# Decayed keys and the diagonal of the first two chunks from the transposed r and k, by TensorE

## The chip, the cores and the metric

The program runs on one core of a Trainium2 chip. The metric is the device time of one execution in microseconds (us), median of several; lower is better. The core has TensorE (PE; its weight loads are PEld), VectorE (DVE), ScalarE (ACT), GpSimd (POOL), and SyncE (SP), which here only issues DMAs. Each engine works through its own instructions in the order in which the program writes them and waits on semaphores for the others.

## The reference

Three blocks in a row, all in float32:

```
# 1: attention with decay; batch 2, heads 8, seq 768, head_dim 48
for t in range(S):
    cur = einsum('bhd,bhe->bhde', u * k_t, v_t)
    y_t = einsum('bhd,bhde->bhe', r_t, state + cur)
    state = w * state + einsum('bhd,bhe->bhde', k_t, v_t)
# 2: mixture of experts on x = y as 1536 tokens x 384; 4 experts, 384 -> 1024 -> 384
p = domain_probs / (domain_probs.sum(-1) + 1e-9)
out = sum over e of p[:, e] * (relu(x @ w1[e]) @ w2[e])
# 3: one layer 384 -> 2048 -> 384 with ELU between
```

## The kernel before

The 1536 tokens are 12 chunks of 128, six for each batch. Of a chunk the kernel holds r and k transposed (`rkT`: 112 partitions, that is two heads of 48 at partitions 0 and 64, by 4 pairs of heads by 128 tokens), and r, k (`rk`) and v with the tokens on the partitions. Two tables of powers of the decay w, `T` and its reciprocal `Kd`, turn r and k into r·wᵗ and k·w⁻ᵗ (`s1h`, DVE, line 200). TensorE forms all products of k' and r' of a chunk (`s2`, line 252), DVE copies those under the mask into the tile `A` (`s2p`, line 259), and the diagonal of `A` is the sum over d of r·u·k for each token and head. In chunks 2 and later POOL writes that diagonal into `A` (`s1d`, line 235); for chunks 0 and 1 `A` holds zeros there, and v times the diagonal (`va`, line 230) is added by a product with the identity (line 362).

`s1u` (lines 217, 219) multiplies r, u and k of `rk` for the diagonal, `s1d` sums it (line 226). `s1k` (line 210) makes the decayed keys `kp` with the tokens on the partitions, from `rk` and `Kt`, the transposed `Kd` (`setup_kt`). `s3u` (line 273) multiplies `kp` with v for the state and `s3s` (lines 294, 296) brings the state forward on DVE. `s3` is the output of chunks 2 and later: a part from the state (line 308), `s3u`, and `A` times v (line 316). Chunks 0 and 1 go by `s3f` (line 359), which yields their outputs transposed, in PSUM, ready for the first layer; `put_x` splits them into a high part (ACT, line 477) and a low part (DVE, line 478).

Each float32 matrix of the layers is split so as well: `split` casts a slice of 128x768 weights on ACT (line 514) and subtracts on DVE (line 515), and then asks for the next load. `work(budget)` runs such pieces, `weights` runs them when one is missing. `layers` runs all experts; expert 0 goes over blocks of 256 tokens, and the attention of chunks 2 to 11 is laid between its steps: a list `steps`, of which `NS[f]` are taken behind step f of the first block. Each step f is: first layer (`st1`, line 664, nine products in 1.08 us), evacuation (`evac`, lines 676 and 677), steps of the list, second layer of the step two before (`st2`, line 702), one piece of `work`. Slice 2 is used first by step f = 2.

Ahead of `layers`, `fast` writes out by hand the order of zeros for TensorE (`warm`), loads, tables and the work on chunks 0 to 2. `probs` (POOL, lines 621 to 624), `probs2` (one reciprocal on DVE, line 629, and a product on POOL), `probs_out` (a transpose on TensorE, a copy, a store `pd`) and `load_pb` (a load of `pd` spread over 128 partitions, `pb`) bring the expert weights; `pb` is used first at line 720, where the results of a block leave PSUM. SP issues nearly all DMAs.

Of the kernel before, what the change touches and what calls it, by code (L numbers as in the profile page):

```python
# [34 lines left out]
WARM = 18  # L35
NS = (3, 1, 1, 1, 1, 1, 1, 2)
# [14 lines left out]
class Fast:  # L51
# [7 lines left out]
    def __init__(self, g, ctx):  # L59
        self.g, nc, tc = g, g.nc, g.tc  # L60
        self.c = ctx.enter_context(tc.tile_pool(name="at_c", bufs=1))
        self.p2 = ctx.enter_context(tc.tile_pool(name="at_2", bufs=2))
        self.p3 = ctx.enter_context(tc.tile_pool(name="at_3", bufs=3))
        self.p4 = ctx.enter_context(tc.tile_pool(name="at_4", bufs=4))
        self.ps = ctx.enter_context(tc.tile_pool(name="at_ps", bufs=1, space=PSUM))
        c = self.c
        self.A = [c.tile([P, 2, NP, P], F32, name=f"A{i}") for i in range(2)]
        self.kp = [c.tile([P, NP, 2, 64], F32, name=f"kp{i}") for i in range(2)]
        self.Sb = [c.tile([P, NP, 2, 64], F32, name=f"S{i}") for i in range(2)]
        self.wd = c.tile([P, NP], F32, name="wd")  # L70
# [3 lines left out]
        self.ub = c.tile([P, DM], F32, name="ub")  # L74
        self.vp = c.tile([P, 112 + 160 * H], F32, tag="xs", name="vp")
        self.Sp = c.tile([P, 96 + 192 * NP], F32, tag="yT", name="Sp")
        self.mask = c.tile([P, P], U8, name="mask")
        self.rkT, self.rk, self.v, self.va, self.pa, self.st = ({} for _ in range(6))
# [42 lines left out]
    def setup_loads(self):  # L121
        g, nc = self.g, self.g.nc
        nc.sync.dma_start(out=self.wd, in_=g.wd)
        for ci in range(2):
            self.load_T(ci)
            self.load_T2(ci, 0)
            self.load_T2(ci, 1)
        self.load_rk(0)
        nc.sync.dma_start(
            out=self.ub,  # L130
            in_=g.u.rearrange("h d -> (h d)").rearrange("(o n) -> o n", o=1).broadcast_to([P, DM]))
        self.load_v(0)
        self.load_rk(1)
        self.load_v(1)

    def setup_tables(self):
        g, nc = self.g, self.g.nc
        c = self.c
        zz = c.tile([P, 32], F32, name="zz")
        wf = c.tile([P, NP], F32, name="wf")  # L140
        nc.vector.memset(zz, 0.0)
        nc.vector.memset(self.T[:, :, 0:1], 1.0)
# [12 lines left out]
    def setup_tables2(self):  # L155
        nc, Kd = self.g.nc, self.Kd
        for n in (16, 32, 64):
            nc.gpsimd.tensor_tensor(
                out=Kd[:, :, n:2 * n], in0=Kd[:, :, 0:n],
                in1=Kd[:, :, n - 1:n].to_broadcast([P, NP, n]), op=ALU.mult)  # L160

    def setup_masks(self):
# [9 lines left out]
    def setup_zeros(self):  # L172
        nc = self.g.nc
        for t in self.A:
            for j in range(2):
                nc.scalar.copy(t[:, j].rearrange("s p t -> s (p t)"), self.zero)
        for i in range(0, self.vp.shape[1], 512):
            t = self.vp[:, i:min(i + 512, self.vp.shape[1])]
            nc.scalar.copy(t, self.zero[:, 0:t.shape[1]])

    def setup_rest(self):
        nc = self.g.nc
        for t in self.kp:
            nc.gpsimd.memset(t.rearrange("t p j d -> t (p j) d")[:, :, D:64], 0.0)
        nc.gpsimd.memset(self.Sp, 0.0)
        for t in self.Sb:
            nc.gpsimd.memset(t, 0.0)
# [35 lines left out]
    def s1d(self, ci):  # L223
        nc = self.g.nc
        a0 = self.p2.tile([P, H], F32, tag="a0", name="a0")
        nc.vector.tensor_reduce(out=a0, in_=self.st[ci]["uk"], axis=AX.X, op=ALU.add)  # L226
        if ci < 2:

# [4 lines left out]
            return  # L233
        for j in range(2):
            nc.gpsimd.tensor_tensor(  # L235
                out=self.A[ci % 2][:, j], in0=self.g.ident.rearrange("s (a t) -> s a t", a=1).to_broadcast([P, NP, P]),
                in1=a0.rearrange("s (p j o) -> s p j o", j=2, o=1)[:, :, j].to_broadcast([P, NP, P]), op=ALU.mult)

# [5 lines left out]
    def s2(self, ci):  # L244
# [4 lines left out]
        for p, j in ([(p, j) for j in range(2) for p in range(NP)] if ci < 2 else  # L249
                     [(p, j) for p in range(NP) for j in range(2)]):  # L250
# [48 lines left out]
    def s3(self, ci, more=False):  # L299
# [11 lines left out]
        pu = self.s3u(ci)  # L311
        for p in range(NP):
# [29 lines left out]
    def s3f(self, ci):  # L342
        g, nc = self.g, self.g.nc
        st = self.st.pop(ci)
        self.px = px = self.bank().rearrange("q (k t) -> q k t", k=4)
        for kk in range(KD):
# [9 lines left out]
            for n in range(max(map(len, ops))):  # L356
                for i, o in enumerate(ops):
                    if n < len(o):
                        nc.tensor.matmul(
                            px[64 * i:64 * (i + 1), kk, :], *o[n], start=not n and not kk, stop=False)  # L360
        for kk in range(KD):
            nc.tensor.matmul(
                px[:, kk, :], self.va[ci][:, kk * P:(kk + 1) * P], g.ident, start=False, stop=kk == KD - 1)

    def s3x(self, ci):
        self.g.put_x(0, ci * P, P, self.px[:, 0:KD, :], self.g.nc.vector)
# [93 lines left out]
class Gen:  # L460
# [11 lines left out]
    def put_x(self, j, o, n, src, eng):  # L472
# [4 lines left out]
        nc.scalar.copy(xh, src)  # L477
        eng.tensor_tensor(out=xl, in0=src, in1=xh.bitcast(F32), op=ALU.subtract)  # L478
# [28 lines left out]
    def split(self):  # L507
# [6 lines left out]
        nc.scalar.copy(hi, t)  # L514
        self.weng.tensor_tensor(out=lo, in0=t, in1=hi.bitcast(F32), op=ALU.subtract)  # L515
# [254 lines left out]
    def setup(self, ctx):  # L770
# [14 lines left out]
        self.later = []  # L785
# [49 lines left out]
    def fast(self):  # L835
        tc, nc = self.tc, self.nc
        with ExitStack() as ctx:
# [4 lines left out]
            at.warm(WARM)  # L842
            at.setup_zeros()
            at.setup_loads()
            dp = self.probs_in()
# [5 lines left out]
            at.setup_rest()  # L851
            at.setup_tables2()

# [6 lines left out]
            at.s1h(0, 0)  # L860
            at.s1h(0, 1)
            at.setup_kt()
            at.s2(0)
            at.s3v(0)
            at.s1h(1, 0)
            at.s1h(1, 1)
            at.s2p(0)
            at.s1u(0, nc.vector)
            at.s1k(0)
            self.probs(dp)  # L870
            at.s1u(1)
# [4 lines left out]
            load(3)  # L876
            at.s1d(0)
            self.probs2(dp)
            at.s2(1)
            pu = at.s3u(0)  # L880
            at.s3f(0)
            at.s2p(1)
            at.s3s(0, pu)
            at.s1k(1)
            at.s1u(2)
            at.load_rk(3)
            at.s1d(1)
            at.s3v(1)
            at.s3x(0)
            at.s1h(2, 0)  # L890
            at.s1h(2, 1)
            self.work(0.1)
            at.nbank = 0
            self.probs_out(at.bank)
            at.nbank = len(at.own)
            at.s3f(1)
            at.nbank = 2
            pu = at.s3u(1)
            at.s3x(1)
            at.s3s(1, pu)  # L900
            at.s1k(2)
            at.s1d(2)
            self.work(0.1)
            at.banks, at.nbank = at.own, 0
            load(4)
            at.load_rk(4)

# [157 lines left out]
```

## Time and profile before

| | |
|---|---|
| median of 3 runs | 658.91 us (658.71 to 659.19) |
| profiled execution | 658.46 us, of which the span from its first to its last instruction is 656.6 us |
| granted TensorE clock, mean | 0.994 of full |
| first product of the layers begins | 19.00 us |
| end of the last product | some 651 us, then evacuation and store |

Times in rows are us from the start of the span. A timeline row has the start, the time from the first start to the last end of the instructions merged in it, the engine, the line, what is written from what, shapes, the count, and in brackets how long the engine had been idle before, and on whom it waited. A busy share tells nothing of the order: the first 50 us, in which the attention, the loads and the splits start together, are read by themselves.

### The profile page before, as it was taken

The numbers are of one execution on the slowest core, as the hardware profiler recorded it, in microseconds if no ns is written. First come the engines' busy times: TensorE is split into PE (matmuls) and PEld (weight loads), VectorE is DVE, ScalarE is ACT, GpSimd is POOL, SyncE is SP. The second block draws the span as 40 slices with busy tenths as digits, with TensorE's granted clock in tenths as the row PEclk, the third lists the DMA queues.
The fourth block names the chain that finished last, engine by engine and source line by source line (L and its number), as shares of the span: only waits on it lengthen the run. The fifth ranks groups of instructions, "written<-read, shape, count | busy, mean of one in ns | idle before, by whom it ended". The sixth has DMA issues, their size and how long they took to land.

```text
span 656.6 us, 8916 instructions
## 1 busy us (share of the span) xinstructions
PE 646.6 (98%) x3563; PEld 545.5 (83%) x3563; DVE 342.1 (52%) x490; ACT 211.9 (32%) x351; POOL 213.1 (32%) x177
## 2 busy tenths in 40 slices
PE   8899999999999999999999999999999999999996
PEld 6799999988888888888888888888888888888885
DVE  7985677245454555554545455566666653112122
ACT  4331222233211123221122112123546464544441
POOL 6755575100012130312130314142764434333331
PEclk8899999999999999999999999999999999999999
DMA  8883661433320214322307132208540342001011
GB/s 251 252 251 138 177 177 50 145 118 99 121 67 29 96 60 158 107 111 96 97 0 265 68 125 97 96 25 311 193 145 26 119 144 97 0 1 48 1 49 53
DMA packets 27876, 73.26 MB, mean 112 GB/s; under 512 B 3170, under 2 KB 8723, under 8 KB 27827
## 3 DMA queue, kind: packets, MB, share of 16 engines
q1 hardware_dynamic: 23072, 60.00, 28.3%
q10 hardware_dynamic: 4754, 12.61, 5.0%
q8 instruction: 30, 0.49, 0.3%
q14 instruction: 20, 0.16, 0.1%
HBM read 55.67 MB, written 16.93 MB: 111 GB/s over the span
## 4 chain that ended last, share of the span: by engine, by line
PE 93%; DMA 2%; DVE 2%; POOL 1%; issue 1%; SPq 0%; ACT 0%; DVEq 0%
PE po L702 45%; PE ph L664 45%; PE pa L316 1%; DMA rk<-in_rkv_dram 1%; DMA ub<-in_u_dram 1%; PE pa L308 1%; PE po L252 1%; POOL A L235 1%; PE pa L252 0%; PE pa L273 0%; DVE acc L752 0%; DVE A L259 0%; POOL uk L217 0%; SPq L110 0%; DVE rkT L200 0%
## 5 line engine op out<-in xcount | busy, mean ns | idle before, releaser
L702 PE MATMUL po<-hh,wh 128*128 128x512 f32 (+1 forms) x480 | 177.4, 370 | 0.0
L702 PE MATMUL po<-hh,wl 128*128 128x512 f32 (+1 forms) x480 | 176.5, 368 | 0.0
L702 PE MATMUL po<-hl,wh 128*128 128x512 f32 (+1 forms) x480 | 176.5, 368 | 0.0
L664 PE MATMUL ph<-xh,wh 128*128 128x512 f32 (+1 forms) x480 | 175.0, 370 | 0.2
L664 PE MATMUL ph<-xh,wl 128*128 128x512 f32 (+1 forms) x480 | 174.4, 369 | 0.2 <-DVE wl L515 0.2
L676 ACT ACTIVATE hh<-ph 128x512 fp32r<-128x512 f32 (+1 forms) x112 | 60.1, 536 | 278.6 <-PE ph L664 275.1
L677 DVE SCALAR_TENSOR_TENSOR hl<-ph,hh 128x512 fp32r<-128x512 f32 (+1 forms) x112 | 68.5, 613 | 154.5 <-ACT hh L676 154.1
L664 PE MATMUL ph<-xl,wh 128*128 128x512 f32 (+1 forms) x480 | 125.0, 369 | 0.0
L664 PEld LDWEIGHTS ph<-xh,wh 128*128 128x128 f32 x480 | 90.8, 189 | 15.9 <-ACT xh L477 0.5
L702 PEld LDWEIGHTS po<-hh,wh 128*128 128x128 f32 x480 | 90.4, 188 | 16.2 <-issue 0.4
L664 PEld LDWEIGHTS ph<-xh,wl 128*128 128x128 f32 x480 | 90.9, 189 | 15.3 <-DVE wl L515 0.4
L702 PEld LDWEIGHTS po<-hl,wh 128*128 128x128 f32 x480 | 90.4, 188 | 15.1
L702 PEld LDWEIGHTS po<-hh,wl 128*128 128x128 f32 x480 | 90.4, 188 | 14.9
L689 POOL TENSOR_TENSOR hl<-g,hh 128x512 fp32r<-128x512 f32 x48 | 63.4, 1321 | 117.0 <-ACT hh L688 108.8
L664 PEld LDWEIGHTS ph<-xl,wh 128*128 128x128 f32 x480 | 86.2, 189 | 15.2 <-DVE xl L478 0.2
L686 DVE SCALAR_TENSOR_TENSOR g<-m,ph 128x512 f32<-128x512 f32 x48 | 33.0, 687 | 105.2 <-ACT m L684 101.0
L577 POOL TENSOR_TENSOR nl<-a,wide 128x768 fp32r<-128x768 f32 x16 | 30.1, 1883 | 173.5 <-DVE a L576 132.6
L724 POOL TENSOR_TENSOR acc<-acc,t 128x512 f32<-128x512 f32 x27 | 34.2, 1294 | 72.9 <-DVE t L723 72.9
L688 ACT CAST hh<-g 128x512 fp32r<-128x512 f32 x48 | 29.8, 622 | 42.9 <-DVE g L686 42.9
L683 ACT ACTIVATE m<-ph 128x512 f32<-128x512 f32 x48 | 28.7, 597 | 43.4 <-PE ph L664 35.9
L515 DVE TENSOR_TENSOR wl<-raw,wh 128x768 fp32r<-128x768 f32 x32 | 31.7, 1002 | 3.4 <-ACT wh L514 2.8
L235 POOL TENSOR_TENSOR A<-ident,a 128x512 f32<-128x512 f32 x20 | 23.1, 1177 | 27.2 <-DVE a L226 26.0
(105 smaller groups left out, 500.4 us busy)
## 6 DMA issues: line engine op xcount, KB each, us to landing
raw<-in_ws_dram SPq DMA_DIRECT2D x32, 384.0 KB, 4.4
wide<-in_ws_dram SPq DMA_DIRECT2D x16, 768.0 KB, 4.9
w<-nh ACTq DMA_DIRECT2D x16, 384.0 KB, 2.3
w<-nl ACTq DMA_DIRECT2D x16, 384.0 KB, 5.6
wh<-w SPq DMA_DIRECT2D x16, 384.0 KB, 5.5
wl<-w SPq DMA_DIRECT2D x16, 384.0 KB, 6.5
rk<-in_rkv_dram SPq DMA_DIRECT2D x12, 384.0 KB, 6.5
rkT<-in_rkT_dram SPq DMA_DIRECT2D x10, 448.0 KB, 6.1
```

Source lines behind the costliest of these rows:

```text
L235: nc.gpsimd.tensor_tensor(out=self.A[ci % 2][:, j], in0=self.g.ident.rearrange("s (a t) -> s a t", a=1).to_broadcast([P, NP, P]), in1=a0.r ...
L515: self.weng.tensor_tensor(out=lo, in0=t, in1=hi.bitcast(F32), op=ALU.subtract)
L577: nc.gpsimd.tensor_tensor(out=lo, in0=af, in1=cf, op=ALU.add)
L664: nc.tensor.matmul(ph[:, 0:n], a[:, kk, c0:c0 + P], b[:, kk], start=q == 0, stop=q == 3 * KD - 1)
L676: nc.scalar.activation(hh[:, 0:n], ph[:, 0:n], AF.Relu)
L677: nc.vector.scalar_tensor_tensor(out=hl[:, 0:n], in0=ph[:, 0:n], scalar=0.0, in1=hh[:, 0:n].bitcast(F32), op0=ALU.max, op1=ALU.subtract)
L683: nc.scalar.activation(m, ph, AF.Relu, scale=-1.0)
L686: nc.vector.scalar_tensor_tensor(out=gg, in0=m, scalar=-1.0, in1=ph, op0=ALU.add, op1=ALU.max)
L688: nc.scalar.copy(hh, gg)
L689: nc.gpsimd.tensor_tensor(out=hl, in0=gg, in1=hh.bitcast(F32), op=ALU.subtract)
L702: nc.tensor.matmul(po, a[:, ff, i * P:(i + 1) * P], b[:, 0:n], start=f == 0 and q == 0 and not i * n % TB, stop=f == NF - 1 and q == 2 and ...
L724: nc.gpsimd.tensor_tensor(out=a, in0=a, in1=t[:, 0:n], op=ALU.add)
```

## The change

- Chunks 0 and 1 no longer load `rk`. Their decayed keys are transposes of k' by TensorE, copied by ACT (`s2k`). Their diagonal: POOL multiplies r' and k' (`s1p`), TensorE multiplies that with u·w (`uw`) into a row for each head (`s2a`), ACT copies it, TensorE turns it back (`s2b`). `kp` of chunk 0 no longer needs `Kt`.
- u comes as one row, spread by a product with ones (`setup_ub`); one more small load, `uf`, stands before the loads of `rkT`.
- `T` is doubled by POOL and `Kd` by DVE, the other way round than before. `A[0]` is cleared by DVE, other clears go from POOL to ACT.
- The order ahead of `layers` is written anew. The loads of chunks 2 and 3 are asked for before the first product; `setup_kt`, `s1k(2)`, `probs` and `probs2` stand behind `s1d(2)`, at the end; `probs_out` moves among the steps, before `load_pb(0)`; the state of chunk 1 (`u1`) moves to the first step, so that `NS[0]` is 4 and not 3. The first slice of weights is split in two pieces and the second slice only in the steps: two slices before, one now.
- Zeros for TensorE: 10 and not 18 at the start, one and two between products of chunks 0 and 1, four and three in `s3` of chunks 2 and 3 (`WAIT`).

```diff
-WARM = 18
-NS = (3, 1, 1, 1, 1, 1, 1, 2)
+WARM = 10
+WAIT = {2: 4, 3: 3}
+NS = (4, 1, 1, 1, 1, 2, 1, 2)
...
         for n in (32, 64):
-            nc.vector.tensor_tensor(
+            nc.gpsimd.tensor_tensor(
                 out=T[:, :, 1 + n:1 + 2 * n], in0=T[:, :, 1:1 + n],
...
         for n in (16, 32, 64):
-            nc.gpsimd.tensor_tensor(
+            nc.vector.tensor_tensor(
                 out=Kd[:, :, n:2 * n], in0=Kd[:, :, 0:n],
...
+    def setup_ub(self):
+        pu = self.bank()
+        nc.tensor.matmul(pu[:, 0:DM], self.one, self.ur, start=True, stop=True)
+        nc.scalar.copy(self.ub, pu[:, 0:DM])
...
+    def s1p(self, ci):
+        self.st[ci]["rp"] = o = self.p2.tile([P, NP, P], F32, tag="rp", name="rp")
+        self.g.nc.gpsimd.tensor_tensor(
+            out=o[0:112], in0=self.st[ci]["r"][0:112], in1=self.st[ci]["k"][0:112], op=ALU.mult)
+    def s2k(self, ci):
+        pk = self.bank().rearrange("t (p n) -> t p n", p=NP)
+        for p in range(NP):
+            nc.tensor.transpose(
+                pk[:, p, 0:112], self.st[ci]["k"][0:112, p, :], self.g.ident[0:112, 0:112])
+        nc.scalar.copy(
+            self.kp[ci % 2].rearrange("t p j d -> t p (j d)")[:, :, 0:112], pk[:, :, 0:112])
+    def s2a(self, ci, pz):
+        rp = self.st[ci].pop("rp")
+        for p in range(NP):
+            nc.tensor.matmul(
+                pz[32 * p:32 * p + 32, ci * P:(ci + 1) * P], self.uw[0:112, p, :], rp[0:112, p, :],
+                start=True, stop=True)
+        self.st[ci]["at"] = t = self.p2.tile([P, P], F32, tag="at", name="at")
+        nc.scalar.copy(t, pz[:, ci * P:(ci + 1) * P])
+    def s2b(self, ci, pz):
+        a0 = pz[:, 2 * P + ci * H:2 * P + (ci + 1) * H]
+        self.g.nc.tensor.matmul(
+            a0.rearrange("t (p j) -> t p j", j=2), self.st[ci].pop("at"),
+            self.g.ident.rearrange("q (p n) -> q p n", n=32)[:, :, 0:2], start=True, stop=True)
+        self.st[ci]["a0"] = a0
...
         pu = self.s3u(ci)
+        for _ in range(WAIT.get(ci, 0)):
+            nc.tensor.matmul(
+                py[0:112].rearrange("q p t -> q (p t)"), self.zero[:, 0:112], self.zero, start=False, stop=False)
...
             at.warm(WARM)
             at.setup_loads()
...
             at.load_T(2)
             at.load_rk(2)
             self.load_next()
             at.load_v(2)
             load(3)
+            at.load_rk(3)
+            at.setup_ub()
+            at.zeros(at.Sp)
+            dp = self.probs_in()
             at.s1h(0, 0)
             at.s1h(0, 1)
             at.s2(0)
+            at.s1p(0)
             at.s1h(1, 0)
             at.s1h(1, 1)
             at.s2p(0)
+            at.s1p(1)
+            at.s2k(0)
+            pz = [at.bank(), at.bank()]
+            at.s2a(0, pz[0])
+            at.s2(1)
+            at.warm(1)
+            at.s2b(0, pz[1])
+            at.s3v(0)
+            at.s2p(1)
+            pu = at.s3u(0)
+            at.zeros_S(1)
             at.s1d(0)
+            at.s3s(0, pu)
+            at.s2a(1, pz[0])
+            self.half = True
+            self.work(0.01)
+            self.half = False
+            at.warm(2)
             at.s3f(0)
+            at.s2b(1, pz[1])
+            at.s3d(0)
             at.s1d(1)
             at.s3v(1)
+            self.work(0.1)
+            at.s3x(0, 0)
+            at.s3f(1)
+            at.s3d(1)
+            at.s3x(0, 1)
+            at.s1u(2)
             at.s1h(2, 0)
             at.s1h(2, 1)
+            at.s3x(1, 0)
+            at.s3x(1, 1)
+            at.s1d(2)
+            at.setup_kt()
+            at.s2k(1)
             at.s1k(2)
+            self.probs(dp)
+            self.probs2(dp)
+            at.zeros_S(0)
...
-            steps = [(lambda c: self.work(0.1), 0)] + [(a1, 2), (a2, 3), (a3, 2), (a1, 3), (a3, 3), (a2, 4)]
-            steps += [(lambda c: self.load_pb(0), 0), (a1, 4), (at.s4, 3)]
+            steps = [(u1, 1), (lambda c: self.work(0.1), 0)] + [(a1, 2), (a2, 3), (a3, 2), (a1, 3), (a3, 3), (a2, 4)]
+            steps += [(lambda c: self.probs_out(at.bank), 0), (lambda c: self.load_pb(0), 0), (a1, 4), (at.s4, 3)]
```

`s3d` is the product of `va` with the identity, taken out of `s3f`; `s3x(c, 0)` is the high part of `put_x` and `s3x(c, 1)` the low part. `s2` of chunks 0 and 1 takes its heads in the order of the later chunks.

## Rows read from the trace of the kernel before

**Rows 1.** Page, part 1: busy us, share of the span, instructions.

```profile
PE 646.6 (98%) x3563; PEld 545.5 (83%) x3563; DVE 342.1 (52%) x490; ACT 211.9 (32%) x351; POOL 213.1 (32%) x177
```

**Rows 2.** Waits of PE, whole span: us in total, times, longest.

```profile
PE pa L316 <- DVE A L259: 2.1, 3, 1.3
```

**Rows 3.** Chain that ended last, first 110 us: start, us, what.

```profile
11.47 7.06 DMA rk<-in_rkv_dram
...
22.58 3.48 POOL A L235 x2
```

**Rows 4.** One stretch of a us: busy by engine, granted PE clock, DMA share, GB/s.

```profile
11.00:12.00 1.00, 1.00 (x22) 1.00 (x21) 0.95 (x2) 0.23 (x1) 0.39 (x1) 0.50 1.05 421
```

**Rows 5.** Timeline of PE.

```profile
10.78 0.88 PE L273 MATMUL po<-v,kp 128*48 128x48 f32 x16 [0.73 <-DMA v<-in_rkv_dram]
11.42 2.83 PE L359 MATMUL ph<-A,vp 128*64 128x128 f32 x24
...
15.15 0.44 PE L359 MATMUL po<-rkT,Sp 112*64 112x128 f32 x4
...
17.49 0.94 PE L362 MATMUL po<-ident,va 128*128 128x128 f32 x6
...
31.73 0.39 PE L702 MATMUL po<-hh,wh 128*128 128x256 f32 x1
...
37.00 0.39 PE L702 MATMUL po<-hh,wh 128*128 128x256 f32 x1
...
43.66 1.16 PE L252 MATMUL pa<-rkT 48*128 48x128 f32 x16
```

**Rows 6.** Timeline of ACT: high part of chunk 1.

```profile
18.46 0.48 ACT L477 CAST xh<-po 128x384 fp32r<-128x384 f32 x1 [1.95 <-PE po L362]
```

**Rows 7.** Timeline of DVE.

```profile
4.33 0.74 DVE L151 TENSOR_TENSOR T<-T 128x128 f32<-128x128 f32 x2
...
6.39 0.69 DVE L200 TENSOR_TENSOR rkT<-rkT,Kd 112x512 f32<-112x512 f32 x1 [0.51 <-POOL Kd L158]
...
12.95 0.21 DVE L629 RECIPROCAL sm<-sm 128x12 f32<-128x12 f32 x1
...
27.48 1.49 DVE L200 TENSOR_TENSOR rkT<-rkT,Kd 112x512 f32<-112x512 f32 x1
```

**Rows 8.** Timeline of POOL.

```profile
4.50 1.85 POOL L158 TENSOR_TENSOR Kd<-Kd 128x64 f32<-128x64 f32 x3 [0.35 <-DVE Kd L149]
8.37 1.00 POOL L210 TENSOR_TENSOR kp<-rk,Kt 128x384 f32<-128x384 f32 x1 [2.02 <-DMA rk<-in_rkv_dram]
9.33 0.23 POOL L621 TENSOR_TENSOR s<-dp 128x24 f32<-128x24 f32 x1
...
9.94 0.24 POOL L624 TENSOR_SCALAR sm<-sm 128x12 f32<-128x12 f32 x1
...
51.11 2.05 POOL L235 TENSOR_TENSOR A<-ident,a 128x512 f32<-128x512 f32 x2 [4.32 <-DVE a L226]
```

**Rows 9.** Groups by form, 0 to 60 us: busy us, mean ns; idle before.

```profile
L515 DVE TENSOR_TENSOR wl<-raw,wh 128x768 fp32r<-128x768 f32 x8 | 9.1, 1143 | 0.1
...
L259 DVE COPY_PREDICATED A<-mask,pa 128x512 f32<-128x512 uint8 x10 | 6.9, 731 | 0.7 <-PE pa L252 0.3 <-POOL A L235 0.3
...
L677 DVE SCALAR_TENSOR_TENSOR hl<-ph,hh 128x256 fp32r<-128x256 f32 x11 | 4.6, 420 | 2.5 <-ACT hh L676 2.4
...
L226 DVE TENSOR_REDUCE a<-uk 128x8 f32<-128x384 f32 x7 | 3.8, 548 | 0.1
L296 DVE TENSOR_TENSOR S<-Z,T 48x192 f32<-48x192 f32 x8 | 3.7, 468 | 0.3
...
L294 DVE TENSOR_TENSOR Z<-po,S 48x192 f32<-48x192 f32 x6 | 2.1, 350 | 0.0
```

**Rows 10.** DMA issues at 42 to 57 us: count, KB, us to landing.

```profile
pb<-pd SPq DMA_DIRECT2D x1, 768.0 KB, 8.7
```

**Rows 11.** DMA issues of the whole span: count, KB, median us to landing.

```profile
pb<-pd SPq DMA_DIRECT2D x4, 768.0 KB, 3.9
```

More of the change, by code (lines that the diff above doesn't have):

```diff
@@ L74, in __init__ @@
         self.ub = c.tile([P, DM], F32, name="ub")
+        self.ur = c.tile([1, DM], F32, name="ur")
+        self.one = c.tile([1, P], F32, name="one")
+        self.uf = c.tile([P, NP], F32, name="uf")
+        self.wf = c.tile([P, NP], F32, name="wf")
+        self.uw = c.tile([P, NP, 32], F32, name="uw")
         self.vp = c.tile([P, 112 + 160 * H], F32, tag="xs", name="vp")
@@ L77, in __init__ @@
         self.mask = c.tile([P, P], U8, name="mask")
-        self.rkT, self.rk, self.v, self.va, self.pa, self.st = ({} for _ in range(6))
+        self.rkT, self.rk, self.v, self.va, self.pa, self.st, self.px = ({} for _ in range(7))
         self.S = self.Sv = self.zero = None
@@ L123, in setup_loads @@
         nc.sync.dma_start(out=self.wd, in_=g.wd)
+        nc.sync.dma_start(out=self.uf, in_=g.ud)
         for ci in range(2):
@@ L127, in setup_loads @@
             self.load_T2(ci, 1)
[L128 to L131, printed above, removed]
         self.load_v(0)
-        self.load_rk(1)
         self.load_v(1)
+        nc.scalar.dma_start(out=self.ur, in_=g.u.rearrange("h d -> (h d)").rearrange("(o n) -> o n", o=1))
     def setup_tables(self):
@@ L139, in setup_tables @@
         zz = c.tile([P, 32], F32, name="zz")
-        wf = c.tile([P, NP], F32, name="wf")
+        wf = self.wf
         nc.vector.memset(zz, 0.0)
+        nc.vector.memset(self.one, 1.0)
         nc.vector.memset(self.T[:, :, 0:1], 1.0)
@@ L150, in setup_tables, with setup_uw @@
         for n in (32, 64):
-            nc.vector.tensor_tensor(
+            nc.gpsimd.tensor_tensor(
                 out=T[:, :, 1 + n:1 + 2 * n], in0=T[:, :, 1:1 + n],
                 in1=T[:, :, n:n + 1].to_broadcast([P, NP, n]), op=ALU.mult)
-    def setup_tables2(self):
-        nc, Kd = self.g.nc, self.Kd
+        Kd = self.Kd
         for n in (16, 32, 64):
-            nc.gpsimd.tensor_tensor(
+            nc.vector.tensor_tensor(
                 out=Kd[:, :, n:2 * n], in0=Kd[:, :, 0:n],
                 in1=Kd[:, :, n - 1:n].to_broadcast([P, NP, n]), op=ALU.mult)
+    def setup_uw(self):
+        nc = self.g.nc
+        for j in range(2):
+            a = slice(64 * j, 64 * (j + 1))
+            nc.gpsimd.tensor_tensor(
+                out=self.uw[a, :, j], in0=self.uf[a], in1=self.wf[a], op=ALU.mult)
+    def setup_ub(self):
+        nc = self.g.nc
+        pu = self.bank()
+        nc.tensor.matmul(pu[:, 0:DM], self.one, self.ur, start=True, stop=True)
+        nc.scalar.copy(self.ub, pu[:, 0:DM])
     def setup_masks(self):
@@ L170, in setup_masks, with zeros, zeros_A, zeros_S @@
         nc.gpsimd.tensor_copy(self.mask, mf)
[L172 to L187, printed above, removed]
+        nc.gpsimd.memset(self.uw, 0.0)
+    def zeros(self, t):
+        for i in range(0, t.shape[1], 512):
+            o = t[:, i:min(i + 512, t.shape[1])]
+            self.g.nc.scalar.copy(o, self.zero[:, 0:o.shape[1]])
+    def zeros_A(self, i):
+        for j in range(2):
+            self.zeros(self.A[i][:, j].rearrange("s p t -> s (p t)"))
+    def zeros_S(self, i):
+        self.zeros(self.Sb[i].rearrange("t p j d -> t (p j d)"))
     def setup_kt(self):
@@ L224, in s1d @@
         nc = self.g.nc
-        a0 = self.p2.tile([P, H], F32, tag="a0", name="a0")
-        nc.vector.tensor_reduce(out=a0, in_=self.st[ci]["uk"], axis=AX.X, op=ALU.add)
         if ci < 2:
+            a0 = self.st[ci]["a0"]
             self.va[ci] = va = self.p2.tile([P, DM], F32, tag="va", name="va")
@@ L233, in s1d @@
             return
+        a0 = self.p2.tile([P, H], F32, tag="a0", name="a0")
+        nc.vector.tensor_reduce(out=a0, in_=self.st[ci]["uk"], axis=AX.X, op=ALU.add)
         for j in range(2):
@@ L248, in s2 @@
         self.pa[ci] = pa = [self.bank().rearrange("q (p t) -> q p t", p=NP) for j in range(2)]
-        for p, j in ([(p, j) for j in range(2) for p in range(NP)] if ci < 2 else
-                     [(p, j) for p in range(NP) for j in range(2)]):
+        for p, j in [(p, j) for p in range(NP) for j in range(2)]:
             a = 64 * j
@@ L343, in s3f @@
         g, nc = self.g, self.g.nc
-        st = self.st.pop(ci)
-        self.px = px = self.bank().rearrange("q (k t) -> q k t", k=4)
+        st = self.st[ci]
+        self.px[ci] = px = self.bank().rearrange("q (k t) -> q k t", k=4)
         for kk in range(KD):
@@ L470, in new_x, with put_x @@
         self.xl[j] = self.xp.tile([P, KD, TB], F32R, tag=f"xl{j}", name=f"xl{j}")
[L472 removed]
+    def put_x(self, j, o, n, src, eng, parts=(0, 1)):
         nc = self.nc
@@ L476, in put_x @@
         xh, xl = self.xh[j][:, :, o:o + n], self.xl[j][:, :, o:o + n]
-        nc.scalar.copy(xh, src)
-        eng.tensor_tensor(out=xl, in0=src, in1=xh.bitcast(F32), op=ALU.subtract)
+        if 0 in parts:
+            nc.scalar.copy(xh, src)
+        if 1 in parts:
+            eng.tensor_tensor(out=xl, in0=src, in1=xh.bitcast(F32), op=ALU.subtract)
     def shape(self, t, kind):
@@ L514, in split @@
         nc.scalar.copy(hi, t)
+        if self.half:
+            yield 0.1
         self.weng.tensor_tensor(out=lo, in0=t, in1=hi.bitcast(F32), op=ALU.subtract)
@@ L784, in setup @@
         self.nwide = self.nnar = self.nget = 0
-        self.later = []
+        self.later, self.half = [], False
         self.add_slots(self.wp, 8)
@@ L841, in fast, with load @@
             at = Fast(self, actx)
+            def load(c):
+                if c < NCH:
+                    at.load_T(c)
+                    at.load_v(c)
             at.warm(WARM)
-            at.setup_zeros()
             at.setup_loads()
-            dp = self.probs_in()
+            nc.vector.memset(at.A[0], 0.0)
+            at.zeros(at.vp)
+            at.zeros_A(1)
             make_identity(nc, self.ident)
@@ L850, in fast @@
             at.setup_tables()
-            at.setup_rest()
-            at.setup_tables2()
-            def load(c):
-                if c < NCH:
-                    at.load_T(c)
-                    at.load_v(c)
[L860 to L871, printed above, removed]
+            at.setup_uw()
             at.load_T(2)
@@ L876, in fast @@
             load(3)
-            at.s1d(0)
-            self.probs2(dp)
-            at.s2(1)
-            pu = at.s3u(0)
-            at.s3f(0)
[L882 to L886, printed above, removed]
+            at.load_rk(3)
+            at.setup_ub()
+            at.zeros(at.Sp)
+            dp = self.probs_in()
+            at.s1h(0, 0)
+            at.s1h(0, 1)
+            at.s2(0)
+            at.s1p(0)
+            at.s1h(1, 0)
+            at.s1h(1, 1)
+            at.s2p(0)
+            at.s1p(1)
[9 more added lines that the diff above has]
+            at.zeros_S(1)
+            at.s1d(0)
+            at.s3s(0, pu)
[4 more added lines that the diff above has]
+            at.warm(2)
+            at.s3f(0)
+            at.s2b(1, pz[1])
+            at.s3d(0)
             at.s1d(1)
             at.s3v(1)
-            at.s3x(0)
+            self.work(0.1)
[4 more added lines that the diff above has]
+            at.s1u(2)
             at.s1h(2, 0)
             at.s1h(2, 1)
[L892 to L900, printed above, removed]
+            at.s3x(1, 0)
[3 more added lines that the diff above has]
+            at.s2k(1)
             at.s1k(2)
-            at.s1d(2)
-            self.work(0.1)
+            self.probs(dp)
+            self.probs2(dp)
+            at.zeros_S(0)
             at.banks, at.nbank = at.own, 0
@@ L906, in fast, with u1 @@
             at.load_rk(4)
+            def u1(c):
+                at.s3s(c, at.s3u(c))
             def a1(c):
```

10 lines of the change are left out of this document (7 added, 3 removed).

## Prediction

> **What bounds the kernel now.** I read the page first: TensorE has instructions running in 98% of the span [rows 1], so over the whole span nothing but its work sets the time. Then the waits of TensorE. The longest group is that of the products of `A` with v for the diagonal [rows 2], all of it in the first 40 us, and from 40 to 655 us the view names no wait of PE at all. So the change can act on the first 40 us only: what it is worth is how much earlier or later TensorE comes to the point from which it no longer waits. My mark for that is the end of `A` times v of chunk 3, where before has line 702 at 37.00 [rows 5]. Behind it both kernels give TensorE nearly the same work.
>
> Then the chain of waits there: a load of `rk` that is let in late, since its buffer is held by an older chunk, POOL's products on it, POOL's diagonal `A` [rows 3], DVE's mask copy, TensorE. [...] Last, the timelines of DVE and POOL, in the order in which the program writes them: what stands in line behind what decides this case.
>
> The profiled execution took 658.46 us, 656.6 of it the span, 0.45 under the median of 658.91. I work out a difference at the mark and add it to the median.
>
> **The head, to the high part of chunk 1.** *Tables.* Before, the second product of `s1h` started at 6.39, after a wait of 0.51 for POOL's `Kd` [rows 7]. Now DVE makes `Kd`: behind the reciprocal at 4.4 come three products of 448 columns in all; two of 384 took 0.74 [rows 7], so about 0.95, to 5.4. POOL makes `T`, 384 columns from 3.9: at least 1.0, as one product of 384 columns, at most 1.6, by 1.85 for 448 [rows 8]; I take 1.35, to 5.3, nearer to the middle since DVE works beside it. Then r' and k' of chunk 0, 0.62 each, are done at 6.7. That is 0.4 us earlier than before. The clear of `A[0]` lies where DVE waits for w; uncovered it would cost about 1 us.
>
> *TensorE from 6.73*, at full clock: products of chunk 0 1.1 (the interleaved order of a later chunk took 1.16 with its tail [rows 5]); four transposes 0.45 (six passes with identity took 0.94 with tail [rows 5]); 0.07 of waiting for POOL's r'k', which is 512 columns from 6.73, between 1.02 by the diagonal alone and 1.74 in the chain [rows 3, 8], taken as 1.56; `s2a` 0.4; products of chunk 1 1.1; a zero 0.22; `s2b` 0.1; `s3u` 0.5 (0.88 at half clock [rows 5]); `s2a` 0.4; two zeros 0.43; `s3f(0)` 1.4, half of the 2.83 at half clock; `s2b` 0.1; `s3d` 0.65; `s3f(1)` 2.34, from 15.15 to 17.49 [rows 5]; `s3d` 0.65. End 16.64. DVE's copies, `va` and `s3s(0)` fit beside it (`va(0)` at 11.8 for 13.0). The high part of chunk 1 starts at 16.7 where before has 18.46 [rows 6]: a gain of 1.75 us. The loads are not the limit: 0.98 MB fewer stand ahead of `rk(2)`, which before was held until 11.47 and landed 7.06 later [rows 3]; it is wanted by 16.2. If it landed at 18.5 as before, all that follows would be 2.4 later; I exclude that, as its buffer is free now.
>
> **Where the gain goes: DVE's line.** In the new order the reciprocal of `probs2` stands on DVE between the sum of chunk 2's diagonal and everything of the layers. It waits for POOL's `probs`, and `probs` stands behind the diagonal of chunk 2 and `kp(2)`. Before, the same reciprocal at 12.95 found its data ready [rows 7]. Step by step: high part 16.7 to 17.18; low part (384 columns, as a sum: 0.55) to 17.79; sum 0.55 [rows 9], to 18.34; POOL's diagonal 2.05, alone as at 51.11, to 20.45; `kp(2)` 1.0; `probs` 0.85, from 9.33 to 10.18 before [rows 8]; so 22.3. DVE stands still for 4 us and has its reciprocal at 22.57. Queued behind it, all needed: low part of hidden 0.42, state of chunk 1 (two of 0.35, two of 0.47) 1.64, slice 1 1.14, mask copy of chunk 2 1.34, r' and k' of chunk 3 1.43 (0.69 to 1.49 each [rows 7]), sum 0.55, slice 2 1.14 [rows 9]: 7.66, to 30.23. Who waits: TensorE, first in `s3` of chunk 2 for the state, from 21.2 until 24.7, and then in step f = 2, whose second product needs the low part of slice 2. Before, the second slice was split earlier, so that slice 2 was there.
>
> The four zeros run from 26.1 to 27.0, while the mask copy ends at 26.9 to 27.1: they cost nothing, and 0.85 if the copy were early. `A` times v ends at 28.1. Then step 2 stands until 30.23; its remaining eight products take 0.95, products of chunk 3 1.08: the second layer's first product comes at 32.3, where before has 31.73 [rows 5]. From there before needed 5.27 to the mark, with 0.6 of waiting in `s3(3)`; now three zeros of 512 columns (0.64 at 2.4 GHz) stand in that place, so 5.2: mark at 37.5.
>
> **Sum:** 37.5 − 37.0 = +0.5 us. Bounds of the unknown costs: with DVE's pieces as short as when POOL is idle (r' and k' 1.25, slices 0.95, state 1.45) 0.8 less, and 0.4 less with the short r'k': −0.7. With POOL's diagonal at 3.48 as in the chain and r' and k' at twice 1.49: +1.4 and +1.5, so +3.4 at most.
>
> *`pd` and `pb`.* `pb` landed 8.7 us after its issue at 45.30, at 54.0, and the first use followed at 54.09; alone it takes 3.9 [rows 10, 11]. Now `pd` must land first, behind the same loads: about 52, then 3.9 for `pb`, 56. Line 720 is then 2 us later. The second block's `st2` at 57.8 needs it 1.1 us of evacuation later, at 57.1: nothing, or up to 1 us. I take nothing. [...]
>
> *Contention.* The POOL diagonal took 3.48 us beside a busy DVE and 2.05 beside an idle one [rows 3, 8]. [...]
>
> **Rivals.**
>
> 1. *Half clock in the head.* Between the ten zeros (end 4.8), the product for u (to 5.4) and the first products at 6.73 PE stands 1.3 us, longer than the 0.73 that went ahead of the half clock of before. For: that row. Against: what follows is denser than before. The stretch of before, 10.9 to 14.1, costs half of its 3.2 us: +1.6, and everything behind is in a chain, so 658.9 + 0.5 + 1.6 = 661.0. The 3.5 us wait before `s3(2)` will surely be followed by half clock too, but there step 2 waits for slice 2 anyway, and it costs 0 to 1.4.
>
> 2. *No standstill of DVE (the other side).* If the reciprocal waited little, DVE would begin the layers' work at 19.4, not 22.6. Then state 21.5, slice 1 22.7, mask copy 23.9, slice 2 27.3, mark 34.7: −2.3, 656.6. For: a wait for something of no urgency would be the first thing to be seen in a profile. Against: the written order, and the rows of before follow the written order on DVE throughout. It decides from a standstill under some 1.6 us on.
>
> 3. *Contention*: diagonal of chunk 2 at 3.48 although DVE is idle, or r' and k' of chunks 1 and 3 at 1.49: +1.4 to +1.5 on top, 660.9.
>
> 4. *`pb` so late that `st2` of the second block waits*: +1 and, with the clock, +1.5: 660.9.
>
> **Chances.** Forecast, head won and lost again to the standstill: 0.40, itself from 658.0 to 660.2. Rival 1 0.20, rival 2 0.27, rival 3 0.08, rival 4 0.05. A change under 0.2% (1.3 us) can't be told from none here. Faster is rival 2, 0.27; slower are rivals 1, 3 and 4, 0.33; the rest is 0.40. Predicted time 658.9 + 0.5 = 659.4. The range goes down to 656.5, which rival 2 reaches, and up to 661.4, which holds rivals 1, 3 and 4 at their worked-out times.
>
> **What would show it.** The first layer product near 17.6 instead of 19.0; line 629 on DVE behind an idle time of about 4 us that ends with POOL's line 624; PE idle about 3.5 us before line 308 of chunk 2, and again before the second product of step 2, for line 515; `A` times v of chunk 3 ending at 37.5. I am wrong if line 629 waits little, if PEclk reads 0.5 in the head, or if a new PE wait shows at 50 to 60 us behind line 720.

## The result and the profile after

The changed kernel takes 664.17 us (median of 6 executions, 661.71 to 665.42) where the kernel before took 658.98 beside it (6 executions, 658.71 to 659.23): ratio 1.0071, 95% interval 1.0058 to 1.0085. It is slower by 5.2 us, the forecast was 659.4, and the range ended at 661.4. Three single executions of later series took 1311 us or more, one each in experiments 2 and 6 and one of the kernel before; no figure for a ratio or a spread below includes them.

The six executions lie in two groups: 661.71 and 662.18 with a mean granted clock of 0.996 and 0.994, and four from 663.98 to 665.42 with 0.989 to 0.991. The profiled one is that of 662.18 us, span 660.3. It lost 3.72 us on the profiled execution of before; the other 1.5 us of the median's loss stand in executions that this profile doesn't show.

Page, busy time and instructions:

```profile
PE 648.1 (98%) x3594; PEld 545.4 (83%) x3595; DVE 339.4 (51%) x489; ACT 214.5 (32%) x358; POOL 207.0 (31%) x172
```

Waits of PE, whole span. Lines have moved: 200 is now 213, 226 is 247, 235 is 249, 252 is 298, 259 is 305, 273 is 319, 296 is 342, 308 is 354, 316 is 366, 359 is 409, 362 is 415, 477 is 531, 515 is 572, 624 is 681, 629 is 686, 664 is 721, 702 is 759, 720 is 777; the zeros stand in 106 and, within `s3`, in 360.

```profile
PE po L354 <- DVE S L342: 3.8, 1, 3.8
...
PE pa L298 <- DVE rkT L213: 0.7, 1, 0.7
PE ph L298 <- DVE rkT L213: 0.2, 1, 0.2
```

One wait of 3.8 us, for the state of chunk 1, stands where before had 2.1 in three pieces [rows 2]. Who was late is seen on DVE and POOL. Timeline of DVE:

```profile
8.08 0.69 DVE L213 TENSOR_TENSOR rkT<-rkT,Kd 112x512 f32<-112x512 f32 x1 [1.04 <-DMA rkT<-in_rkT_dram]
...
23.13 0.23 DVE L686 RECIPROCAL sm<-sm 128x12 f32<-128x12 f32 x1 [3.99 <-POOL sm L681]
...
25.28 0.67 DVE L342 TENSOR_TENSOR S<-Z,T 48x192 f32<-48x192 f32 x1
...
26.97 1.34 DVE L305 COPY_PREDICATED A<-mask,pa 128x512 f32<-128x512 uint8 x2
...
29.86 0.95 DVE L572 TENSOR_TENSOR wl<-raw,wh 128x768 fp32r<-128x768 f32 x1
```

Timeline of POOL in that standstill:

```profile
19.29 2.04 POOL L249 TENSOR_TENSOR A<-ident,a 128x512 f32<-128x512 f32 x2 [1.88 <-DVE a L247]
21.29 1.01 POOL L223 TENSOR_TENSOR kp<-rk,Kt 128x384 f32<-128x384 f32 x1
...
22.86 0.24 POOL L681 TENSOR_SCALAR sm<-sm 128x12 f32<-128x12 f32 x1
```

DVE stood for 3.99 us before a reciprocal of 12 elements, where before it found its data ready [rows 7]. Behind it came the state of chunk 1, done at 25.95. What TensorE did from there, as its timeline, and the granted clock in two of the stretches (columns as in [rows 4]):

```profile
26.10 2.02 PE L354 MATMUL po<-rkT,S 112*112 112x128 f32 x8 [3.77 <-DVE S L342]
28.05 0.88 PE L319 MATMUL pa<-v,kp 128*48 128x48 f32 x16
28.86 1.96 PE L360 MATMUL po<-zero 128*112 128x512 bf16 x4
30.75 1.35 PE L366 MATMUL po<-A,v 128*48 128x128 f32 x16
...
38.11 0.85 PE L360 MATMUL po<-zero 128*112 128x512 bf16 x3
38.89 1.08 PE L366 MATMUL po<-A,v 128*48 128x128 f32 x16
```

```profile
25.00:26.00 1.00, 0.00 (x0) 0.00 (x0) 0.93 (x3) 0.00 (x0) 0.74 (x1) 0.50 0.00 0
28.00:29.00 1.00, 1.00 (x18) 0.86 (x18) 1.00 (x3) 0.00 (x0) 0.00 (x0) 0.50 0.91 286
```

While TensorE stood and while it then worked the clock read 0.50, from 24.5 to 31.3. Four zeros took 1.96 us there and three took 0.85 at full clock. The timeline gives the second layer's first product and, behind `A` times v of chunk 3, the mark:

```profile
34.38 0.39 PE L759 MATMUL po<-hh,wh 128*128 128x256 f32 x1
...
39.90 0.39 PE L759 MATMUL po<-hh,wh 128*128 128x256 f32 x1
```

They are at 34.38 and 39.90, where before has 31.73 and 37.00 [rows 5]. So 2.90 of the 3.72 us are lost at the mark, and 0.82 behind it.

The total of half clock doesn't tell the two profiles apart. Before has the stretch from 10.8 to 14.2 [rows 4] and a second one, from 27.9 to 31.3, behind its own waits for the mask copy [rows 2], which is not among the rows:

```profile
28.00:29.00 1.00, 1.00 (x5) 1.00 (x6) 1.00 (x2) 0.97 (x2) 0.41 (x1) 0.50 0.93 305
```

That makes 6.8 us in either kernel, and a mean of 0.994 in both. What differs is what TensorE does in them: before it works throughout, now it stands for 1.6 us of them and runs zeros for 1.9.

### The profile page after: what moved, and what is told of

It reads as the page before. It is cut to its first block, busy times and chain, and to the rows that moved or that the text cites. A ratio compares the mean times of both kernels' runs of the same rounds, so it can differ in the third digit from the quotient of the medians.

```text
span 660.3 us, 8975 instructions
## 1 busy us (share of the span) xinstructions
PE 648.1 (98%) x3594; PEld 545.4 (83%) x3595; DVE 339.4 (51%) x489; ACT 214.5 (32%) x358; POOL 207.0 (31%) x172
## 4 chain that ended last, share of the span: by engine, by line
PE 96%; DVE 1%; DMA 1%; POOL 1%; SPq 0%; ACT 0%; issue 0%; POOLq 0%
PE ph L721 45%; PE po L759 45%; PE pa L298 1%; PE po L366 1%; PE po L354 1%; DMA rkT<-in_rkT_dram 1%; PE pa L319 1%; PE po L360 0%; PE po L409 0%; DVE acc L809 0%; POOL A L249 0%; PE pa L366 0%; PE pa L354 0%; DVE S L342 0%; PE pa L409 0%
```

## Experiments

Each ratio is to the kernel before, run on the same chip. In the three series (experiments 1 to 4, 5 to 8 and 9 to 12) the kernel before itself took 658.95, 659.25 and 659.02 us in the median, with single executions from 657.73 to 662.44. The theories: **A**, the standstill of DVE costs the time; **B**, the clock in the head does, through fewer zeros at the start; **C**, the zeros in `s3` of chunks 2 and 3 lengthen the path; **D**, the second slice, split late, does.

**1. `probs` and `probs2` early (in the changed kernel).**

```diff
             at.s2p(0)
+            self.probs(dp)
             at.s1p(1)
...
             at.s1d(1)
+            self.probs2(dp)
             at.s3v(1)
...
-            self.probs(dp)
-            self.probs2(dp)
```

> probs goes behind r'k' of chunk 1 on POOL (idle there from 10.2 to 15.0) and probs2 behind the diagonal of chunk 1 on DVE; nothing else moves. Theory A (DVE's standstill of 4 us behind the diagonal of chunk 2, and the half clock that PE's wait of 3.8 us brings, are the loss): DVE goes on at 19.2, PE waits under 2 us for the state of chunk 1, no half clock near 25 to 31, the end of A times v of chunk 3 comes near 35 and not 40, time 656 to 659. Theory B (the loss is half clock and late loads in the head, ahead of 18 us): the time stays within 1 us of the changed kernel, since the standstill only takes the place of other waits.

661.28 us, 1.0031 [1.0014, 1.0048]: 2.9 less than the changed kernel. DVE no longer waits for POOL, and the wait for the state shrinks to 0.5. Waits of PE:

```profile
PE ph L721 <- DVE wl L572: 1.1, 1, 1.1
PE po L354 <- DVE S L342: 0.5, 1, 0.5
```

The twelve executions fall into three equal groups: 659.0 to 659.7 (clock 0.997 to 0.999), 661.0 to 661.4 (0.993, once 0.997) and 662.9 to 663.3 (0.998). The profile, of 661.38, is of the middle group. Its clock falls in the head, and the high part of chunk 1 comes 3.1 us later than in the changed kernel's profile:

```profile
9.00:10.00 1.00, 1.00 (x12) 1.00 (x14) 1.00 (x2) 1.00 (x3) 1.00 (x1) 0.54 1.08 389
```

```profile
20.69 0.48 ACT L531 CAST xh<-po 128x384 fp32r<-128x384 f32 x1 [2.73 <-PE po L415]
```

The stretch behind it runs at full clock now (1.00 in each us from 16 on). The same products as from 26.10 in the changed kernel, four zeros included, take 4.0 us and not 6.0:

```profile
25.86 1.10 PE L354 MATMUL po<-rkT,S 112*112 112x128 f32 x8 [0.46 <-DVE S L342]
...
27.38 1.07 PE L360 MATMUL po<-zero 128*112 128x512 bf16 x4
28.38 1.50 PE L366 MATMUL po<-A,v 128*48 128x128 f32 x16
```

The zeros end at 28.45 there and the mask copy at 28.76, so that at full clock they cost nothing. So A holds, and something in the head scatters the time by up to 4 us: B is alive.

**2. No zeros in `s3` of chunks 2 and 3.**

```diff
-WAIT = {2: 4, 3: 3}
+WAIT = {}
```

> The seven zeros in s3 of chunks 2 and 3 are left out. Theory C (they run at half clock, 1.9 us for four, behind the mask copy that is done by 28.3, and three more cost 0.8 where nothing is waited for): 1.5 to 2 us less than the changed kernel. The other view (they keep the clock up): the half clock lasts longer than to 31.3 or comes again, and the time is the same or more.

663.14 us, 1.0055 [1.0036, 1.0074]. Its lowest three are 660.19 to 660.78, where the changed kernel's lowest two are 661.71 and 662.18: about 1.5 us less. PE timeline:

```profile
26.34 2.02 PE L354 MATMUL po<-rkT,S 112*112 112x128 f32 x8 [3.79 <-DVE S L342]
28.29 0.88 PE L319 MATMUL pa<-v,kp 128*48 128x48 f32 x16
28.96 1.91 PE L366 MATMUL po<-A,v 128*48 128x128 f32 x16
```

`A` times v follows with nothing in between and ends at 30.87 and not 32.10; the mark is at 38.22, 1.68 earlier, although the head was 0.22 later. C holds: the seven zeros cost that, in this place. Of it 0.76 stand at the second layer's first product (33.62), since step 2's products then began at half clock (1.72 us from 30.81 to the products of chunk 3, for 1.26 in the changed kernel), and 0.92 come from the three zeros of chunk 3. The half clock lasted as long without them, 6.8 us, from 24.9 to 31.8.

**3. 18 zeros at the start again.**

```diff
-WARM = 10
+WARM = 18
```

> 18 zeros at the start as before, not 10: they fill TensorE until 6.5. Theory B (executions at 664 to 665 have half clock in the head as well, from the gaps at 4.8 to 6.5): all executions near 662, spread under 1 us, mean granted clock 0.994 or more. Theory A: the median falls by what those executions have too much, but not under 661.5; the best execution is not better than 661.7.

663.60 us (662.98 to 664.85), 1.0074 [1.0050, 1.0097]. No half clock in the head of the profiled execution (1.00 in each us up to 25), and the scatter falls from 3.7 us to 1.9 in five executions. But the first products begin at 7.85, behind the zeros and the product for u, and not at 6.45, and the high part of chunk 1 comes at 18.62, as late as before's 18.46 [rows 6]. The median was expected near 662: what is gained in the clock is lost in the later start.

**4. The second slice split early.**

```diff
+            self.work(0.1)
             self.probs(dp)
```

> The second slice is split ahead of probs2, in DVE's standstill, as the kernel before split two slices ahead of the layers. Theory D, the step of the forecast (step 2 waits for slice 2): 1.1 us less. Theory C (PE at half clock comes to step 2 later than the slice): slice 2 is ready by 29.7 instead of 30.8, PE gets there at 32.1 anyway, gain under 0.3 us.

663.56 us (662.87 to 667.81), 1.0083 [1.0053, 1.0112]: no gain clear of the scatter. The slice fills 1.3 us of the standstill, but POOL's diagonal beside it takes 2.76 and not 2.04 us, the reciprocal comes at 24.08 and not 23.13, and the wait of PE for the state grows from 3.8 to 4.5. Timeline of POOL:

```profile
19.53 2.76 POOL L249 TENSOR_TENSOR A<-ident,a 128x512 f32<-128x512 f32 x2 [1.96 <-DVE a L247]
```

D falls, as long as the standstill is there.

**5. `uf` loaded behind `rkT`.**

```diff
-        nc.sync.dma_start(out=self.uf, in_=g.ud)
         for ci in range(2):
...
             self.load_T2(ci, 1)
+        nc.sync.dma_start(out=self.uf, in_=g.ud)
```

> The small load uf is asked for behind the four loads of rkT instead of ahead of them. Theory L (late loads are a term: r' and k' of chunk 1 waited 1.04 us for the fourth piece of rkT, and the high part of chunk 1 starts at 17.6 where the forecast had 16.7): the wait falls to some 0.5, the high part of chunk 1 starts near 17.1, 0.5 us less in executions with the same clock. Rival: the fourth piece lands when the bytes ahead of it are through, so the order of a 2 KB load changes nothing.

664.00 us, 1.0072 [1.0049, 1.0095]: no gain. Now `uf` is late, `uw` and r'k' on POOL with it, and TensorE waits 1.2 us for r'k'. The late piece was exchanged for another one, and TensorE had stood only 0.15 us for the first.

**6. Experiments 1, 2 and 5 together.**

> Three mends together: probs and probs2 early, uf behind rkT, no zeros in s3. Theories A, C and L add up: executions with full clock in the head at 657.5 to 658.7, under the kernel before; those with half clock in the head 2 us above. If the head's clock is what remains (theory B), the executions still fall in two groups.

660.43 us, 1.0015 [1.0003, 1.0027], from 658.08 to 661.90. Its profile is that of the lowest execution, with full clock in the head and the mark at 35.68: 1.3 us earlier than before's, of which 0.4 reach the time (658.08 for 658.46). Full clock in the head was expected to give 657.5 to 658.7, and this execution has it; whether the others, up to 661.90 and in no clear groups, differ by the head's clock isn't shown.

**7. Four more zeros in the head, with experiment 1.**

```diff
             at.setup_ub()
+            at.warm(4)
```

> As e1 (probs and probs2 early), and four more zeros between the product for u and the first products of chunk 0, where TensorE stands for 0.7 us. Theory B (the groups at 661 to 663 come from half clock in the head, brought by that gap): no execution with half clock near 9.5 to 15.5, mean granted clock 0.997 or more throughout, one group at 659 to 660. Rival: the gap isn't what brings it (products of few rows and columns around 7 to 10 are), and the groups stay.

659.59 us, 1.0015 [0.9998, 1.0031]. Nine executions lie between 658.80 and 660.23, two at 665.28. The profile is of one of the two. PE timeline, and a stretch of the head:

```profile
1.17 4.45 PE L106 MATMUL ph<-zero 128*128 128x512 bf16 x10 [1.17 <-DVE zero L103]
...
8.94 2.08 PE L298 MATMUL pa<-rkT 48*128 48x128 f32 x16
```

```profile
10.00:12.00 2.00, 2.00 (x18) 1.50 (x20) 0.95 (x2) 0.00 (x1) 0.39 (x1) 1.00 1.01 244
```

The 16 products of chunk 0 took 2.08 us, where 1.16 is the full pace [rows 5], and products ran like that to about 20 us; the high part of chunk 1 came at 24.66. Yet the clock column reads 1.00, and TensorE nowhere stood for longer than 1.2 us: the pace must be read beside the column. The one group that B expected at 659 to 660 came for nine of eleven executions.

**8. The standstill in the kernel before.**

```diff
-            self.probs(dp)
...
-            self.probs2(dp)
...
             at.s1d(2)
+            self.probs(dp)
+            self.probs2(dp)
```

with `probs_out` among the steps, as the change has it.

> The kernel before, with only this moved: probs and probs2 behind the diagonal of chunk 2 and its decayed keys, probs_out among the steps ahead of load_pb(0). Theory A: DVE stands still for 4 to 5 us at line 629 here too, PE waits for the mask copy of chunk 2 and goes to half clock, and the time rises by 3 us or more, to 662 or above. Theory B: the standstill is taken up by waits that are there anyway, under 1 us.

661.67 us, 1.0032 [1.0022, 1.0042]: this move alone costs 2.1 to 2.4 us in the kernel before, less than the 3 expected. Wait of PE, followed by half clock from 28.6 to 35.5:

```profile
PE pa L316 <- DVE A L259: 4.5, 1, 4.5
```

**9. Experiment 1 without zeros in `s3`, with 18 zeros at the start, `uf` issued by ACT, and the product for u in the place of a zero behind `s2(1)`.**

```diff
-WARM = 10
-WAIT = {2: 4, 3: 3}
+WARM = 18
+WAIT = {}
...
-        nc.sync.dma_start(out=self.uf, in_=g.ud)
+        nc.scalar.dma_start(out=self.uf, in_=g.ud)
...
-            at.setup_ub()
...
-            at.warm(1)
+            at.setup_ub()
```

> Mended from what the runs show: probs and probs2 early; uf asked for by ACT; no zeros in s3; 18 zeros at the start and the product for u behind the products of chunk 1, in the place of one zero. Theories A and B: no half clock after the first 4.5 us, PE waits under 1 us for the state and about 1.1 us for slice 2, the end of A times v of chunk 3 near 35.5, all executions in one group at 657.3 to 658.7, a little under the kernel before. If the head's clock has another cause, the executions still lie 2 to 4 us apart.

659.34 us, 1.0002 [0.9992, 1.0013], from 657.66 to 661.19, where one group at 657.3 to 658.7 was expected; half clock from 11.1 to 14.5 in its profile, and 1.1 us of waiting for the low part of slice 2.

**10. The same, with the first slice split whole, so that two are split early.**

```diff
-            self.half = True
-            self.work(0.01)
-            self.half = False
+            self.work(0.1)
```

> As e10, and the first slice is split whole ahead of the layers' first work, so that two slices are split ahead of the layers as in the kernel before. Theory D (slice 2 is late): PE's wait of 1.1 us in step 2 goes, 0.5 to 1.1 us less than e10, 656.5 to 658. Rival: DVE is the bound of this stretch, the piece only moves, and what follows on DVE comes later: within 0.3 us of e10.

658.52 us (657.77 to 658.87 in 11 executions), 0.9984 [0.9974, 0.9994]: by the medians 0.5 us under the kernel before, by the interval 0.4 to 1.7, and 5.7 under the changed one. All clocks are 0.997 to 0.999. Waits of PE, and the high part of chunk 1:

```profile
PE po L366 <- DVE A L305: 1.5, 4, 0.8
PE ph L106 <- DVE zero L103: 1.2, 1, 1.2
PE po L354 <- DVE S L342: 0.6, 1, 0.6
```

```profile
19.18 0.48 ACT L531 CAST xh<-po 128x384 fp32r<-128x384 f32 x1 [2.59 <-PE po L415]
```

The wait for slice 2 is gone, and no half clock shows. The head itself is later than before's 18.46, and the mark, at 36.70, is 0.3 earlier: what this version wins, it wins behind the head. Against experiment 9, though, the profiles give D nothing: the mark is 0.63 earlier and the head 0.68, since TensorE now waits for the mask copy of chunk 3:

```profile
35.08 0.42 PE L366 MATMUL po<-A,v 128*48 128x128 f32 x2 [0.37 <-DVE A L305]
```

From the second layer's first product to the mark it takes 5.78 us and in experiment 9 4.60. So the wait moved, as the rival had it, and in the profiles the gain is the head's.

**11. The changed kernel with 18 zeros and the product for u later.**

> The changed kernel with 18 zeros at the start, and the product for u behind the products of chunk 1. Theory B: what the executions of the changed kernel lose beyond 662 goes, all within 661.3 to 662.7, median 2 us under the changed kernel; the standstill of 4 us and the half clock from 25 to 31 stay. Rival: the head's clock depends on the thin products of chunks 0 and 1, and groups stay.

663.41 us (663.10 to 664.05), 1.0062 [1.0049, 1.0076]. The scatter falls to 1 us in five executions; the wait of 3.8 and the half clock behind it (26.3 to 33.2) stay, and the lowest execution stays 4 us over the kernel before's median. B expected 2 us less than the changed kernel, and it is 0.8: the head is later, with the high part of chunk 1 at 18.94 and not 17.61.

**12. The kernel before with 10 zeros.**

```diff
-WARM = 18
+WARM = 10
```

> The kernel before with 10 zeros at the start instead of 18. Theory B (ten zeros don't always bring the clock up, nor hold it to the first products): a second group of executions 1 to 4 us above 659, or all up by 1 us. Rival (the zeros at the start don't matter, since before has half clock at 11 to 14 anyway): 658.5 to 659.5 as the kernel before.

660.98 us, 1.0024 [1.0012, 1.0037], from 659.51 to 662.54: fewer zeros cost the kernel before 0.8 to 2.4 us too. The profile is of the slowest execution, PE timeline:

```profile
1.17 4.45 PE L100 MATMUL ph<-zero 128*128 128x512 bf16 x10 [1.17 <-DVE T L142]
...
8.39 2.45 PE L252 MATMUL pa<-rkT 48*128 48x128 f32 x13
```

Again half pace from the start (the same 13 products take 1.37 us in the profile of before), with a clock column that reads 1.00 and a mean of 0.999. So of the three groups in experiment 1 the highest, at 0.998, is likely this form of the head, and the middle one that in which the pace comes up and the clock then falls; only the middle one was profiled there.

## Why the prediction was wrong

**Right: the standstill.** Forecast 4 us on line 629, measured 3.99; reciprocal done at 22.57, measured 23.36. Experiments 1 and 8 show what it costs, half clock behind it included, from either side: 2.9 us taken away and 2.1 to 2.4 added. Rival 2, that it wouldn't happen, falls. In the 3.99 us before the reciprocal DVE began nothing of what stands behind it in the program, although TensorE's products for the state of chunk 1 (line 319) had ended at 19.97.

**Wrong: "there step 2 waits for slice 2 anyway, and it costs 0 to 1.4".** I saw that half clock would follow the wait and put it at nothing, because slice 2 was to hide it until 30.23. The low part of slice 2 was ready at 30.81, near the forecast. But state part, `s3u`, four zeros and `A` times v took 6.0 us, from 26.10 to 32.10, and not 3.4. PE had become the later one by 1.3 us, and the cover was gone. Two pieces make it: state part and `s3u` took 2.8 for 1.4, and the zeros, "they cost nothing", took 1.96 and not 0.85, while the mask copy, done at 28.3, no longer hid them. Experiment 2 shows the term of the zeros. That half clock is what stretches the path is seen beside experiment 1, where the same products at full clock take 4.0 us and the zeros are hidden; it couldn't be taken away with the wait left in place. The cover was thin besides: 6.0 us from the forecast's own 24.7 end at 30.7, 0.5 behind its 30.23. The state then came 1.4 later than that, and this fell on TensorE in full.

**Mis-sized: terms before and behind it.** The high part of chunk 1 came at 17.61, not 16.7. The fourth piece of `rkT` landed at 8.06 and line 213 waited 1.04 for it, where I had written "the loads are not the limit" with `rk(2)` alone in view. But TensorE stood only 0.15 us for it and began chunk 1's products at 8.83, where the sum has 8.75. The rest grew behind that, on TensorE: in its chain of waits `s3f(0)` took 1.53 for 1.4, the second `s2b` 0.32 for 0.1, the two `s3d` 0.77 and 0.88 for 0.65 each. POOL's r'k' took 1.65 and 1.31 for my 1.56. From the reciprocal's end to the state it took 2.59, not 2.06. From the second layer's first product to the mark it took 5.52, not 5.2; without the three zeros there it took 4.60 (experiment 2). The 0.64 us that the forecast gave those zeros was worked out from a clock rate in GHz, which no run shows; in the runs they took 0.85 from the first one's start to the last one's end, and leaving them out gained 0.92. And "behind it both kernels give TensorE nearly the same work" missed 0.82 us: the time less the mark is 621.46 before, 622.28 after, and 622.32 and 622.31 in experiments 1 and 2. Of that, 0.33 lie on TensorE between the mark and the end of its last product (614.41 for 614.08); what made them wasn't tried. The other 0.49 lie behind that product, 7.87 us for 7.38. Over all profiles this tail is 7.38 to 8.52, and 8.30 for the kernel before with ten zeros: it scatters, and isn't shown to be the change's.

**Under-weighted: rival 1.** I gave half clock in the head 0.20. By their mean clock it came in four of six executions. I argued from the row of 0.73 us of standing [rows 5] and against it from denser work behind; I never priced the removal of eight zeros as such. Experiment 12 does, on before alone: 2 us of median. Of the changed kernel itself no execution with half clock in the head was profiled. That its upper four are of that kind is argued from their mean clock: 0.990 for 0.995 of 660 us is an estimate of 6.6 us more at half clock, which is worth up to 3.3 us, and they lie 2.6 us higher; and from the profiles of experiments 1 and 5, where the stretch stands in the head (9.1 to 15.9 us and 10.9 to 14.3). Where it stands in those four isn't shown.

**The sum of the error.** Forecast +0.5 against a measured +5.2 at the median: 2.4 at the mark (half clock over the path and its zeros, late head), 0.8 behind the mark, and the last 1.5 from executions with, by their mean, more half clock than the profiled one. The range ended at 661.4 although the sum's own upper bound was +3.4, so 662.3: it held each rival alone, and not two together.

**Right, with nothing to pay.** `T` and `Kd` swapped: the second product of `s1h` starts at 5.71, 6.39 before. In part this is luck: `Kd` took DVE 1.43 us for my 0.95, but began at 3.76 and not 4.4. Rival 3: POOL's diagonal took 2.04, not 3.48, with DVE standing still; the 2.76 of experiment 4 is what the same two products take with DVE at work on a slice. Rival 4: `pd` and `pb` landed 6.3 and 5.5 us after their issues, `pb` at 59.4 and not 56, and PE shows no wait behind line 777.

**What stays open.** What decides in one execution whether TensorE's pace comes up in the ten zeros, comes up and the clock then falls, or the pace doesn't come up until 20 us: the runs show that 18 zeros with no late product behind them leave one narrow group when the standstill is gone too (experiment 10), and not why. In experiment 9, with the same 18 zeros, the profile still had a half-clock stretch; what the whole first slice changes there, beyond the wait of 1.1 us that it removes, isn't settled. The intervals of experiments 9 and 10 overlap. Theory D, that the late second slice costs time, is shown nowhere: in experiment 4 the slice brought no gain, and in experiment 10 the wait moved to the mask copy.

## What to carry to other kernels

Look at every instruction that waits for another engine and ask what is queued behind it on its own: a reciprocal of 0.2 us that nobody needs for 30 us held DVE for 4 us, then TensorE for 3.8, and TensorE's clock read 0.50 for 6.8. When a cost is hidden by something that is late, compute both at full clock and at half, zeros included: the four zeros that cost nothing at full clock, in 1.07 us (experiment 1), took 1.96 at 0.50. And when warm-up work is cut, price the cut by itself, over several executions, before the order behind it is judged.

## What the runs showed of the hardware that was not expected

The ten zeros took from 3.73 to 4.45 us in profiles of the same head: some 0.43 us from one to the next throughout in the longest, 0.43 at first and some 0.2 at the last in the shortest. So the moment at which the pace comes up differs between executions, and the clock column reads 1.00 in both. In experiments 7 and 12 the pace did not come up before about 20 and 17 us of the span, with the clock column at 1.00; in 7 TensorE was busy all that time from 1.17 on, in 12 it stood once, for 1.73 us. In experiment 7, 16 products took 2.08 us that take 1.16 elsewhere, under a column of 1.00: the column alone doesn't tell the pace. In experiment 10 TensorE stood for 0.75 us before 26.95 and the clock stayed at 1.00, while before a wait of 0.73 was followed by 0.50 [rows 4, 5]: the length of a wait alone doesn't tell whether the clock falls.
